# Fold matrix first on ScalarE's DMA queue, transposes of the state vectors behind the third fold tile

## The chip, the core and the metric

The kernel runs on one core of a Trainium2 chip. The metric is device time in microseconds (us) for one execution. The kernel before takes 340.8 us (median of 4 runs, 340.13 to 341.16).

## What is computed

Two mixers read the same input `x` (2048 x 1024, bf16), and a sigmoid gate blends their outputs.

```python
g = sigmoid((x * gate_w).sum(-1, keepdims=True))
# A: filter in the spectrum of both axes
a = irfft2(rfft2(x) * (w_r + 1j * w_i))
# B: diagonal complex state space over the sequence
dt = exp(log_dt);  Lam_bar = exp(dt * Lam)
Bu = x @ (((Lam_bar - 1) / Lam)[:, None] * Bmat).T
h[t] = Lam_bar * h[t - 1] + Bu[t]
b = 2 * (h @ Cmat.T).real + x * Dskip
out = g * a + (1 - g) * b
```

## The kernel before

All Fourier transforms are matrix products on TensorE (PE). The work falls into four stages.

**Fold, 0 to 27 us.** `x` comes in eight tiles of 512 KB on SyncE's queue (`load_x`, L208; called xt or CT in the profile). `fstage(jj)` (L467) handles one tile: VectorE (DVE) makes four sums and differences (L471 to L474, tile `eo`), GpSimd (POOL) fixes one column with four small instructions (L476 to L479). After every odd tile, PE multiplies the last two tiles by the fold matrix `FW_sb` in four fold tiles `ps_f` (L498 and L499, 16 column blocks with half of the sums each; a fold tile is eight matmuls of 256 columns), and ScalarE (ACT) copies each fold tile out in two instructions (L502, L503). So there are 16 fold tiles and 32 copies. `ps_f` has three buffers in PSUM.

**Scalars, beside the fold.** The state-space part needs small vectors (decay, angle, input scale). `vec8` holds the four vectors as 8 x 128; four PE transposes (L258, with `ident`) turn them into `vps`, and DVE copies them to `vec` and `gw1` (L272, L274). The generator `scalars()` (L307, `chain`) then runs eight short steps of instructions on 128 x 8 elements, mostly on DVE: step 1 has two exponentials and two sines on ACT, step 7 the Arctan (L351), step 8 `beta` (L355). Step 1 is emitted before the fold; then each `fstage` emits one more. When the steps are done, `tables(q)` (L369) makes the cosine and sine tables, the first of them from L377 to L390.

**Spectrum and state space, 27 to 156 us.** `fft_main` (L642) goes over 16 frequency groups (`fd`, `bf_w`, `w_mul`, `bi`), then does the inverse transforms; `ssm_all` (L736) is merged into it by hand.

**Output, to the end.** The product with `Cmat` (L836), the gate and the store.

The order on SyncE and GpSimd is the program's (`manual_schedule`, L190). On PE, DVE and ACT a planner sets the order beforehand, from estimated durations and from the emission order; on the chip each engine then works strictly in that order. Buffers are rings: tiles with the same tag share `bufs` slots, and a new tile waits until the slot's last reader is done. `vec8` and the `eo` of odd tiles share the tag "cu" with two slots, in the order `vec8`, `eo` of tile 1, `eo` of tile 3.

ScalarE's queue issues six loads at the start: `ident`, the four vectors, and `FW_sb` last (L194 to L198). The loads of both queues share eight completion semaphores in rotation; a load that gets a used semaphore waits on its queue until the earlier load with it has landed. The state-space weights come by DMA transposes (`load_BT`, `load_xT`), which start after a marker copy on DVE (L723) behind tile 3.

Of the kernel before, what the change touches and what calls it, by code (L numbers as in the profile page):

```python
# [22 lines left out]
P = 128  # L23
TC = 512
# [113 lines left out]
def kernel(  # L138
# [52 lines left out]


    FW_sb = BT[:, 7, 0, 0:4, :].rearrange("p a c -> p (a c)")
    nc.scalar.dma_start(out=ident, in_=cId)  # L194
    vec8 = rp.tile([8, 4, P], BF16, name="vec8", tag="cu")
    for i, src in enumerate((B_Lambda_re, B_Lambda_im, B_log_dt, gate_w)):
        nc.scalar.dma_start(out=vec8[:, i, :], in_=src.rearrange("(j p) -> j p", p=P))
    nc.scalar.dma_start(out=FW_sb, in_=cFW)  # L198

    warm = BT[:, 6, 0, 0:4, :].rearrange("p a c -> p (a c)")  # L200
    nc.vector.memset(warm, 0.0)
# [51 lines left out]
    xts.append(load_x(6))  # L253
    load_W(0)
    xts.append(load_x(7))
    vps = psU.tile([P, 4, 8], BF16, name="vps", tag="psu")
    for i in range(4):
        nc.tensor.transpose(out=vps[:, i, :], in_=vec8[:, i, :], identity=ident[0:8, 0:8])  # L258

    sp = cpool  # L260

# [7 lines left out]
        return scr[:, scr_n[0] - 1, :]  # L269

    vec = scr[:, 28:31, :]
    nc.vector.tensor_copy(out=vec, in_=vps[:, 0:3, :])  # L272
    gw1 = sp.tile([P, 8], BF16, name="gw1")
    nc.vector.tensor_copy(out=gw1, in_=vps[:, 3, :])  # L274
    gf = sp.tile([P, 16], FP32, name="gf")
    om_f = sp.tile([P, 16], FP32, name="om_f")
    lre, lim, ldt = vec[:, 0, :], vec[:, 1, :], vec[:, 2, :]
# [80 lines left out]
        yield  # L358

    chain = scalars()  # L360
    for _ in range(1):
        next(chain, None)

    tau_i = rp.tile([P, TC], I32, name="tau_i", tag="su")
    nc.gpsimd.iota(tau_i, pattern=[[1, TC]], base=0, channel_multiplier=0)
# [3 lines left out]
    def tables(q):  # L369
        xa = rp.tile([P, 2 * TC], FP32, name="xa", tag="cu")  # L370
        kk = rp.tile([P, 2 * TC], FP32, name="xa_k", tag="su")
        tq = tab[:, 2 * q:2 * q + 2]
        for jj in range(2):
            jb = 2 * q + jj
            xj, kj = xa[:, TC * jj:TC * (jj + 1)], kk[:, TC * jj:TC * (jj + 1)]
            if q < 1:
                nc.vector.tensor_scalar(out=xj, in0=tau_f, scalar1=thp[:, jb:jb + 1], scalar2=beta[:, jb:jb + 1],  # L377
                                        op0=ALU.mult, op1=ALU.add)
                yield
            else:  # L380
                nc.scalar.activation(out=xj, in_=tau_f, func=ACT.Identity, scale=thp[:, jb:jb + 1],
                                     bias=beta[:, jb:jb + 1])
            nc.vector.tensor_scalar(out=kj, in0=xj, scalar1=MAGIC, scalar2=-MAGIC, op0=ALU.add, op1=ALU.add)
            yield
            nc.vector.tensor_sub(out=xj, in0=xj, in1=kj)
            nc.vector.tensor_scalar(out=kj.bitcast(I32), in0=xj.bitcast(I32), scalar1=0x7FFFFFFF, scalar2=None,
                                    op0=ALU.bitwise_and)
            yield
            nc.scalar.activation(out=tq[:, jj, 0, :], in_=kj, func=ACT.Sin, scale=-TWO_PI_LO, bias=chpi)
            nc.scalar.activation(out=tq[:, jj, 1, :], in_=xj, func=ACT.Sin, scale=-TWO_PI_LO)  # L390
        nc.vector.tensor_scalar_mul(out=tq[:, :, 2, :], in0=tq[:, :, 1, :], scalar1=-1.0)
        yield


# [72 lines left out]
    def fstage(jj):  # L467
        xt = xts[jj]
        eo = (rp if jj % 2 else up).tile([P, 2, 2, 2, 256], BF16, name="eo", tag="cu" if jj % 2 else "u")
        if jj not in ():  # L470
            nc.vector.tensor_add(out=eo[:, :, 0, 0, :], in0=xt[:, :, 0:256], in1=xt[:, :, 512:768])  # L471
        nc.vector.tensor_sub(out=eo[:, :, 1, 0, :], in0=xt[:, :, 0:256], in1=xt[:, :, 512:768])  # L472
        nc.vector.tensor_add(out=eo[:, :, 0, 1, 1:256], in0=xt[:, :, 511:256:-1], in1=xt[:, :, 1023:768:-1])  # L473
        nc.vector.tensor_sub(out=eo[:, :, 1, 1, 1:256], in0=xt[:, :, 511:256:-1], in1=xt[:, :, 1023:768:-1])  # L474
        om = sm.tile([P, 2, 1], FP32, name="om")
        nc.gpsimd.tensor_add(out=eo[:, :, 0, 1, 0:1], in0=xt[:, :, 256:257], in1=xt[:, :, 768:769])  # L476
        nc.gpsimd.tensor_sub(out=om, in0=xt[:, :, 256:257], in1=xt[:, :, 768:769])
        nc.gpsimd.tensor_sub(out=eo[:, :, 1, 1, 0:1], in0=om, in1=eo[:, :, 1, 0, 0:1])
        nc.gpsimd.tensor_add(out=eo[:, :, 1, 0, 0:1], in0=om, in1=eo[:, :, 1, 0, 0:1])  # L479
        eos[jj] = eo  # L480
        for _ in range(1):
            next(chain, None)
        if jj % 2 == 0:
            return
        j0 = 2 * jj - 2
        for eo_i in range(2):
            for b in range(2):
                ps = psF.tile([P, 4, 2, P], FP32, name="ps_f", tag="ps")
                bs = slice(P * b, P * (b + 1))
                for jl in range(4):  # L490
                    jt = jj - 1 + jl // 2
                    v = eos[jt][:, jl % 2, eo_i]
                    if jt in () and eo_i == 0:
                        los = [xts[jt][:, jl % 2, 512 * h + P * b:512 * h + P * (b + 1)] for h in range(2)]
                    else:
                        los = [v[:, 0, bs]]
                    for i, lo in enumerate(los):
                        nc.tensor.matmul(ps[:, jl], lhsT=lo, rhs=FW_sb[:, 0:2 * P], start=(i == 0), stop=False)  # L498
                    nc.tensor.matmul(ps[:, jl], lhsT=v[:, 1, bs], rhs=FW_sb[:, P * (1 + eo_i):P * (3 + eo_i)],  # L499
                                     start=False, stop=True)  # L500
                q = 4 * eo_i + 2 * b
                nc.scalar.copy(out=FX[:, q, :, j0:j0 + 4], in_=ps[:, :, 0, :].rearrange("p j c -> p c j"))  # L502
                (nc.vector.tensor_copy if (jj, eo_i, b) in () else nc.scalar.copy)(  # L503
                    out=FX[:, q + 1, :, j0:j0 + 4], in_=ps[:, :, 1, :].rearrange("p j c -> p c j"))
                yield 1.0
# [110 lines left out]

    def gates():
        pg = psU.tile([P, TC], FP32, name="pg", tag="psu")
        gwT = fr.tile([P, 8, 32], BF16, name="gwT", bufs=1)
        nc.gpsimd.tensor_copy(out=gwT, in_=gw1.unsqueeze(2).to_broadcast([P, 8, 32]))  # L620
        for dblk in range(8):
            for c in range(NCH):
                nc.tensor.matmul(pg[32 * c:32 * (c + 1), :], lhsT=gwT[:, dblk, :], rhs=xT[:, dblk, TC * c:TC * (c + 1)],  # L623
                                 start=(dblk == 0), stop=(dblk == 7))
        lrow = fr.tile([P, 2, TC], BF16, name="lrow", bufs=1)
        nc.scalar.copy(out=lrow[:, 0, :], in_=pg)
        nc.vector.tensor_sub(out=lrow[:, 1, :], in0=pg, in1=lrow[:, 0, :])
        yield
        pc = psU.tile([P, 4, 4], FP32, name="pc", tag="psu")
        for q in range(4):  # L630
            for i in range(2):
                nc.tensor.matmul(pc[:, q, :], lhsT=lrow[:, i, P * q:P * (q + 1)], rhs=ident[:, 0:P:32],
                                 start=(i == 0), stop=(i == 1))
        gb = fr.tile([P, 16], BF16, name="gb", bufs=1)
        nc.scalar.activation(out=gb.rearrange("p (c q) -> p q c", q=4), in_=pc, func=ACT.Sigmoid)
        nc.vector.tensor_copy(out=gf, in_=gb)
        ob = fr.tile([P, 16], BF16, name="ob", bufs=1)
        nc.vector.tensor_scalar(out=ob, in0=gb, scalar1=-1.0, scalar2=1.0, op0=ALU.mult, op1=ALU.add)
        nc.vector.tensor_copy(out=om_f, in_=ob)
        yield  # L640

    def fft_main():  # L642
# [8 lines left out]
        for g in range(16):  # L651
            if g + 2 < 16:
                fd(g + 2)
                yield 1.2
            if g + 1 < 16:
                bf_w(g + 1)
                yield 1.0
            if 1 == 0 and g + 1 < 16:
                w_mul(g + 1)
            bi(g)  # L660
            if 1 == 1 and g + 1 < 16:
                w_mul(g + 1)
            if g + 4 < 16:
                load_M(g + 4)
            for f in sp_work.get(g, ()):
                f()
            yield 1.2
# [4 lines left out]
        for jj in range(9):  # L672
            if jj < 8:
# [6 lines left out]
                def mk_pm():  # L680
                    pm = fr.tile([P, 2, 2, 512], BF16, name="pm")
                    nc.vector.tensor_add(out=pm[:, :, 0, :], in0=yps[:, :, 0, :], in1=yps[:, :, 1, :])
                    nc.vector.tensor_sub(out=pm[:, :, 1, :], in0=yps[:, :, 0, :], in1=yps[:, :, 1, :])
                    pms[jj] = pm

                if -1 < 0 or jj == 0:
                    mk_pm()
                if jj == 5:
                    gt = gates()
                    next(gt)  # L690
                    yield 2.0
                if jj == 5 + 1:
                    next(gt)
                    yield 0.3
            if jj > 0:
# [204 lines left out]
```

## Time and profile before

| what | value |
|---|---|
| median of 4 runs | 340.8 us |
| the profiled execution's own time | 340.91 us |
| its span, first to last instruction | 339.0 us |
| PE busy | 321.3 us, 95% |
| DVE busy | 285.6 us, 84% |
| ACT busy | 191.3 us, 56% |
| POOL busy | 52.2 us, 15% |
| mean granted PE clock | 0.989 |

The span is what the profile's lines add up to; the 1.9 us between it and the execution's own time lie before the first and after the last instruction. Times in the lines count from the start of the span. A line of the timeline gives the start, the duration (instructions of one engine are pipelined, so durations overlap), engine, line, operation, tiles, and in brackets the idle time before it with what ended it. A "q" behind an engine marks its sequencer, such as the issue of a DMA.

### The profile page before, as it was taken

To read this page: it belongs to the slowest core of one execution; us is meant where nothing else is said; L and a number is where in the kernel's file an instruction comes from. 1 tells how busy PE (TensorE), PEld (TensorE's weight loads), DVE (VectorE), ACT (ScalarE), POOL (GpSimd) and SP (SyncE) were. 2 spreads that over 40 slices of the span, in tenths; PEclk is the share of its full clock that TensorE was granted. 3 is DMA by queue.
4 is the path that set the end of the run, shared out by engine and by line. 5 is a ranking of instruction groups with operands and counts; after the bars stand their busy time and mean duration, and the time that the engine had idled before them with its cause. 6 is when DMAs were issued, how large, how long until landed. Compare 5 with 4: busy or idle time off the path is not lost.

```text
span 339.0 us, 4984 instructions
## 1 busy us (share of the span) xinstructions
PE 321.3 (95%) x1813; PEld 174.7 (52%) x1845; DVE 285.6 (84%) x416; ACT 191.3 (56%) x269; POOL 52.2 (15%) x100
## 2 busy tenths in 40 slices
PE   6989989989979999999999999999999999999995
PEld 2765666756646566554444444444444444444442
DVE  4892799999979997999998999999999988972311
ACT  1999899989886877697252425341424425352200
POOL 4540322221301000000011002112022022111100
PEclk9899999999997999999999999999999999999999
DMA  7999999997597113023995054955675283977511
GB/s 253 383 181 232 182 253 194 226 233 151 152 203 142 62 62 126 31 95 140 241 217 178 21 166 82 259 96 131 148 155 145 74 218 95 258 223 228 159 48 45
DMA packets 70712, 54.97 MB, mean 162 GB/s; under 512 B 52768, under 2 KB 57888, under 8 KB 70688
## 3 DMA queue, kind: packets, MB, share of 16 engines
q1 hardware_dynamic: 64144, 38.75, 45.0%
q0 software_dynamic: 6192, 15.74, 21.2%
q8 instruction: 14, 0.23, 0.3%
q10 hardware_dynamic: 352, 0.17, 0.2%
q14 instruction: 10, 0.08, 0.1%
HBM read 21.61 MB, written 8.39 MB: 88 GB/s over the span
## 4 chain that ended last, share of the span: by engine, by line
PE 68%; issue 15%; DMA 7%; POOL 4%; DVE 3%; DVEq 0%; POOLq 0%
PE psy L836 32%; PE psu L412 26%; PE ps_id L589 5%; DMA W<-in_A_w_i_dram 4%; POOL W L246 4%; DMA xt<-in_A_x_dram 3%; PE ps_y L608 1%; PE ps_y L611 1%; PE ps_y L610 1%; PE ps_y L609 1%; DVE eo L471 1%; PE pg L623 1%; DVE eo L472 0%; DVE t L555 0%; DVE eo L473 0%
## 5 line engine op out<-in xcount | busy, mean ns | idle before, releaser
L412 PE MATMUL psu<-xT,BT 128*128 128x512 bf16 x489 | 117.2, 382 | 1.4 <-DMA xT<-in_A_x_dram 0.3
L412 PEld LDWEIGHTS <-BT 128*128 128x128 bf16 x512 | 50.2, 98 | 55.5 <-issue 1.8
L432 DVE TENSOR_TENSOR_SCAN su<-r_sb,carry,cu 128x512 bf16<-128x512 f32 x48 | 57.8, 1266 | 0.4
L414 ACT ACTIVATE u<-psu,rho 128x512 bf16<-128x512 f32 x32 | 22.1, 691 | 50.9 <-PE psu L412 48.4
L414 ACT ACTIVATE u<-psu,nrho 128x512 bf16<-128x512 f32 x32 | 22.1, 692 | 37.4 <-PE psu L412 37.4
L836 PEld LDWEIGHTS <-h 128*128 128x128 bf16 x256 | 25.0, 98 | 30.2
L843 DVE SCALAR_TENSOR_TENSOR o<-psy,om_f,xf 128x1024 bf16<-128x1024 f32 (+1 forms) x17 | 20.6, 1216 | 17.3 <-PE psy L836 17.3
L821 POOL DMA_DIRECT2D xf<-gac x16 | 16.3, 1019 | 118.0 <-ACT xf L820 118.0
L836 PE MATMUL psy<-big,h 128*128 128x512 bf16 x127 | 28.9, 379 | 0.1
L836 PE MATMUL psy<-CT,h 128*128 128x512 bf16 x125 | 28.6, 379 | 0.1
L818 ACT ACTIVATE gac<-gac,gf 128x1024 bf16<-128x1024 bf16 x16 | 18.2, 1140 | 17.6 <-DMA gac<-ya_scratch 17.6
L423 DVE TENSOR_TENSOR cu<-u,tab 128x2048 bf16<-128x2048 bf16 x16 | 19.5, 1218 | 2.3 <-ACT u L414 2.3
L814 DVE TENSOR_TENSOR xc<-xc,dsk_bc 128x1024 bf16<-128x1024 bf16 x16 | 10.9, 684 | 12.0 <-DMA xc<-in_A_x_dram 11.9
L836 PEld LDWEIGHTS <-xT 128*128 128x128 bf16 x128 | 12.5, 98 | 15.1
L836 PEld LDWEIGHTS <-big 128*128 128x128 bf16 x128 | 12.5, 98 | 15.1
L427 DVE TENSOR_TENSOR cu<-cu,su 128x2048 bf16<-128x2048 bf16 x16 | 19.6, 1228 | 0.4
L425 DVE TENSOR_TENSOR su<-u,tab 128x2048 bf16<-128x2048 bf16 x16 | 19.5, 1217 | 0.0
L515 PE MATMUL ps_d<-G_sb,big 128*128 128x256 bf16 (+3 forms) x128 | 18.9, 285 | 0.2 <-ACT X L542 0.2
L432 DVE TENSOR_TENSOR_SCAN su<-r_sb,cu 128x512 bf16<-128x512 f32 x16 | 18.7, 1209 | 0.1
L820 ACT ACTIVATE xf<-xc,om_f 128x1024 f32<-128x1024 bf16 x16 | 18.2, 1139 | 0.4 <-DVE o L843 0.4
L582 ACT CAST big<-ps_q 128x1024 bf16<-128x1024 f32 x16 | 16.3, 1021 | 2.9 <-PE ps_q L581 2.8
L589 PE MATMUL ps_id<-G_sb,big 128*128 128x256 bf16 (+3 forms) x128 | 17.4, 287 | 0.0
(169 smaller groups left out, 576.6 us busy)
## 6 DMA issues: line engine op xcount, KB each, us to landing
xf<-gac POOLq DMA_DIRECT2D x16, 512.0 KB, 6.2
ya_scratch<-ya SPq DMA_DIRECT2D x16, 256.0 KB, 2.0
xc<-in_A_x_dram SPq DMA_DIRECT2D x16, 256.0 KB, 3.8
gac<-ya_scratch SPq DMA_DIRECT2D x16, 256.0 KB, 3.7
out_dram<-o SPq DMA_DIRECT2D x15, 256.0 KB, 2.7
MM<-c_MM SPq DMA_DIRECT2D x16, 192.0 KB, 3.1
xt<-in_A_x_dram SPq DMA_DIRECT2D x4, 512.0 KB, 4.6
CT<-in_A_x_dram SPq DMA_DIRECT2D x4, 512.0 KB, 8.2
```

What stands on the lines that cost most here:

```text
L412: nc.tensor.matmul(psu, lhsT=BT[:, jb, ri, dblk, :], rhs=xT[:, dblk, TC * c:TC * (c + 1)], start=(dblk == 0), stop=(dblk == 7))
L414: nc.scalar.activation(out=u[:, jj, ri, :], in_=psu, func=ACT.Copy, scale=(nrho if ri else rho)[:, jb:jb + 1])
L423: nc.vector.tensor_mul(out=cu, in0=u, in1=tq[:, :, 0:1, :].to_broadcast(full))
L425: nc.vector.tensor_mul(out=su, in0=u[:, :, ::-1, :], in1=tq[:, :, 1:3, :])
L427: nc.vector.tensor_add(out=cu, in0=cu, in1=su)
L432: nc.vector.tensor_tensor_scan(out=su[:, jj, ri, :], data0=r_sb[:, jb:jb + 1].to_broadcast([P, TC]), data1=cu[:, jj, ri, :], initial=(0.0 ...
L515: nc.tensor.matmul(ps[:, lo:lo + w], lhsT=FX[:, q, 8 * g:8 * g + 8, :], rhs=G_sb[:, o:o + w], start=start, stop=stop, skip_group_check=True)
L589: nc.tensor.matmul(ps[:, lo:lo + w], lhsT=FX[:, q, :, j], rhs=G_sb[:, o:o + w], start=start, stop=stop, skip_group_check=True)
L818: nc.scalar.activation(out=gac, in_=gac, func=ACT.Copy, scale=gf[:, tb:tb + 1])
L820: nc.scalar.activation(out=xf, in_=xc, func=ACT.Copy, scale=om_f[:, tb:tb + 1])
L836: nc.tensor.matmul(psy[:, ds], lhsT=hs[c, jb // 2][:, jb % 2, ri, P * tq:P * (tq + 1)], rhs=CT[dh][:, jb, ri, :], start=(i == 0), stop=(i ...
L843: nc.vector.scalar_tensor_tensor(out=o[:, ds], in0=psy[:, ds], scalar=om_f[:, tb:tb + 1], in1=xfs[tb][:, ds], op0=ALU.mult, op1=ALU.add)
```

## The change

Two moves, with a third that follows from the second. The load of `FW_sb` becomes the first of the six on ScalarE's queue. The four transposes and the two copies behind them go into a function `vectors()`, which is called in `fstage(1)` after the third of its four fold tiles; `issue_after` ties the transposes behind that tile's last matmul on PE. The steps of `scalars()` are redistributed: step 1 right behind `vectors()`, then two at tile 2, two at tile 3, one each at tiles 4, 5 and 6.

```diff
     FW_sb = BT[:, 7, 0, 0:4, :].rearrange("p a c -> p (a c)")
+    nc.scalar.dma_start(out=FW_sb, in_=cFW)
     nc.scalar.dma_start(out=ident, in_=cId)
...
         nc.scalar.dma_start(out=vec8[:, i, :], in_=src.rearrange("(j p) -> j p", p=P))
-    nc.scalar.dma_start(out=FW_sb, in_=cFW)
...
-    vps = psU.tile([P, 4, 8], BF16, name="vps", tag="psu")
-    for i in range(4):
-        nc.tensor.transpose(out=vps[:, i, :], in_=vec8[:, i, :], identity=ident[0:8, 0:8])
...
-    nc.vector.tensor_copy(out=vec, in_=vps[:, 0:3, :])
     gw1 = sp.tile([P, 8], BF16, name="gw1")
-    nc.vector.tensor_copy(out=gw1, in_=vps[:, 3, :])
+
+    def vectors():
+        vps = psU.tile([P, 4, 8], BF16, name="vps", tag="psu")
+        for i in range(4):
+            nc.tensor.transpose(out=vps[:, i, :], in_=vec8[:, i, :], identity=ident[0:8, 0:8])
+        nc.vector.tensor_copy(out=vec, in_=vps[:, 0:3, :])
+        nc.vector.tensor_copy(out=gw1, in_=vps[:, 3, :])
...
     chain = scalars()
-    for _ in range(1):
-        next(chain, None)
...
         eos[jj] = eo
-        for _ in range(1):
+        for _ in range((0,0,2,2,1,1,1,0)[jj]):
             next(chain, None)
...
+                if jj == 1 and 2 * eo_i + b == 2:
+                    with tc.issue_after(last.ins):
+                        vectors()
+                    next(chain, None)
```

Everything else in the diff leaves the program as it is: conditions that are never or always true (`q >= 9`, `-1 >= 0`, `-1 < 0`, `if 0`), and two tiles of 16 columns, `gb` and `ob`, in another pool.

## The prediction

> **What bounds the kernel now.** I read the page first: PE is 95% busy over the span, so only time in which PE waits can be won, and that lies before 100 us. Then the table of windows over the fold, and over the stage behind it.
>
> ```profile
> 4.75:6.78 2.03, 0.70 (x4) 0.46 (x5) 1.43 (x4) 0.00 (x0) 1.27 (x4) 1.00 1.04 350
> 6.78:8.12 1.34, 0.95 (x6) 0.48 (x5) 1.33 (x6) 0.21 (x1) 0.99 (x4) 0.79 1.10 349
> 8.12:10.87 2.75, 2.75 (x13) 1.90 (x14) 2.19 (x12) 1.87 (x4) 2.32 (x8) 0.50 0.95 370
> 10.87:12.88 2.01, 1.64 (x14) 1.32 (x13) 1.93 (x9) 2.00 (x6) 1.59 (x6) 0.97 0.99 379
> 12.88:21.26 8.38, 8.31 (x68) 6.27 (x67) 7.84 (x42) 7.76 (x16) 3.62 (x16) 1.00 1.26 273
> 21.26:27.10 5.84, 4.55 (x36) 3.46 (x37) 4.87 (x13) 5.84 (x14) 0.97 (x4) 1.00 1.07 225
> 60.00:80.00 20.00, 18.37 (x141) 12.39 (x143) 19.86 (x37) 18.05 (x26) 5.83 (x10) 1.00 0.97 216
> ```
>
> The columns are length, then busy us and count of PE, PEld, DVE, ACT and POOL, granted clock, DMA share, GB/s. From 10.87 to 27.10 ACT is busy 15.60 of 16.23 us: the fold is ACT's. Before 8.12 ACT does next to nothing. From 60 to 80 DVE has 99%, PE 92%, ACT 90%: an order in which the three hand work to each other, so a shift of its start should run through it.
>
> Next, the timelines of ACT, PE and DVE and the DMA issues say what holds ACT back.
>
> ```profile
> 2.83 0.36 ACTq L198 DMA_DIRECT2D BT<-c_FW  x1
> 8.98 0.59 ACT L502 CAST big<-ps_f 128x512 bf16<-128x512 f32 x1 [1.76 <-PE ps_f L499]
> 10.17 1.28 ACT L313 ACT_TABLE_LOAD   x1
> 21.26 0.21 ACT L351 ACTIVATE scr<-scr 128x8 f32<-128x8 f32 x1 [0.62 <-DVE scr L349]
> 27.09 0.83 ACT L389 ACTIVATE tab<-xa_k,chpi 128x512 bf16<-128x512 f32 x1
> ```
> ```profile
> 6.16 0.60 PE L258 MATMUL vps<-ident,vec 8*128 8x8 bf16 x3 [1.15 <-DMA vec<-in_B_Lambda_im_dram]
> 6.78 0.38 PE L498 MATMUL ps_f<-BT,eo 128*128 128x256 bf16 x2
> 26.58 0.81 PE L412 MATMUL psu<-xT,BT 128*128 128x512 bf16 x2 [0.34 <-DMA xT<-in_A_x_dram]
> ```
> ```profile
> 4.90 0.42 DVE L471 TENSOR_TENSOR eo<-xt 128x512 bf16<-128x512 bf16 x1 [3.78 <-DMA xt<-in_A_x_dram]
> 6.79 0.18 DVE L272 CAST scr<-vps 128x24 f32<-128x24 bf16 x1 [0.46 <-PE vps L258]
> 10.78 0.43 DVE L471 TENSOR_TENSOR eo<-xt 128x512 bf16<-128x512 bf16 x1 [0.56 <-DMA xt<-in_A_x_dram]
> 22.59 0.99 DVE L377 TENSOR_SCALAR xa<-tau_f,ang,beta 128x512 f32<-128x512 f16 x2
> ```
> ```profile
> BT<-c_FW ACTq DMA_DIRECT2D x1, 128.0 KB, 3.9
> ident<-c_ident ACTq DMA_DIRECT2D x1, 32.0 KB, 3.5
> SPq L213 <- DMA ident<-c_ident: 2.7, 1, 2.7
> ```
>
> The fold matrix is issued at 2.83 and lands 3.9 us later, at 6.73; the first fold matmul runs at 6.78, though its sums were there at 4.90 + 0.42 = 5.32. Two gates stand side by side: the matrix, and the transposes until 6.76. The change lifts both. The last line is a wait of SyncE's own queue: the third x tile waits for the semaphore of `ident`.
>
> **The matrix first.** Issued at 0.72, it lands at 0.72 + 3.9 = 4.6 at its own latency; at `ident`'s 3.5, at 4.2. Both are ahead of 5.32, so the first matmul goes at about 5.35, 1.4 us earlier. The other half of the first fold tile needs tile 1's sums. DVE comes to those at 6.96, after the vector copies and 0.46 us of waiting for them; without these it goes on after tile 0, at 4.90 + 4 x 0.34 = 6.26, if tile 1 is there: issued at 1.18, about 5.0 to land, 6.2. So tile 1 and the end of the first fold tile move 0.7 us. ACT's first copy moves from 8.98 to between 8.0 and 8.3; I take 8.0, from the later rows' spacing of a fold tile, 8 x 0.109 us.
>
> The price is on the DMA side. 128 KB now runs beside x tile 0; at the 350 GB/s of the first window that is 0.37 us on its landing at worst, nothing at best, since the same bytes were moved by 6.73 anyway. SyncE's third x tile now waits for the matrix's semaphore instead of `ident`'s: it goes out at 4.2 to 4.6 instead of 4.28, 0 to 0.3 us. I take 0.1 of both, as tile 3, which DVE awaits at 10.78, is behind the same total of bytes.
>
> [...]
>
> **The transposes behind the third fold tile.** They cost PE 0.60 us for three, so 0.8 for four; PE is not the bound of the fold, and these 0.8 us delay only the fourth fold tile, which waits on ACT anyway. What they release comes later: `vec` at 6.97 becomes `vec` after the third fold tile. When that is depends on the clock. At full clock fold tiles 2 and 3 end at 8.0 + 2 x 0.87 = 9.7 and `vec` is there at 10.7. At half clock, as from 8.12 to 10.87, a matmul takes 0.213 us, a tile 1.7, the third ends near 11.0 and `vec` comes at 12.0.
>
> [...] I count nothing for it, and put 13 matmuls x 0.104 = 1.35 us into the low end.
>
> **The scalar steps.** Step 1 is 8 small DVE instructions with the two copies: between wide instructions each shifts the stream by 0.08 us, in series by 0.2, so 0.65 to 1.6 us. Before, they fill DVE's pauses (0.46 at 6.79, 0.56 at 10.78); now they fall behind tile 3, where DVE is busy to 22.6 without a break. The cover is ACT: DVE's first table input is done at about 25.8 and the first sine starts at 27.09, when ACT has finished the copies, 1.3 us of slack. I take 0.8, which it covers. ACT's own work is the same: the table load of 1.28 moves from 10.17 to a place where ACT waits for tile 3's sums. SyncE waits for nothing new on this side; POOL's L319 and L320 stand behind tile 2 instead of tile 0.
>
> **The sum**, on the profiled execution: first copy 8.98 to 8.0, -1.0; DMA +0.1; DVE's delay 0, covered; transposes 0, covered. ACT's end of the fold goes from 27.1 to 26.2. Then xT, which lands at 26.5, is next: PE's product L412 waited 0.34 for it, but the spectrum's `fd` does not need it, and ACT is full from 27 on. I pass on the whole 0.9, and 0.2 more for DVE's two pauses, which leave the stream of tiles 1 and 2. 340.91 - 1.1 = 339.8, and against the median of 340.8, 0.1 below that execution, 339.7.
>
> **Rivals.**
> 1. *Slower: tile 3 waits for `vec8`.* `eo` of tile 3 takes `vec8`'s slot, so its first DVE instruction waits for the last transpose. It decides if that ends after 10.78, so at the half clock: 11.0 + 0.8 = 11.8, DVE stands 1.0 us, and step 1's 0.65 to 1.6 come on top. DVE's stream ends 1.7 to 2.6 late; the Arctan, already 0.62 late in ACT's queue, holds the last six fold tiles' copies behind it. Less the 0.9 won: +0.8 to +1.7, 341.6 to 342.5; with the planner's order against it, 343. For it: the 0.50 clock in the row. Against: ACT may have the later tiles' copies placed ahead of the Arctan.
> 2. *No change: the transfers set the end of the fold.* The DMA share is about 1 throughout; xT lands at 26.5 and tile 3 at 10.76 whatever ACT does. The gain ends in a wait for them, 0 to -0.5: 340.5. The case that the matrix still lands after 6.5, in the crowd of the first loads, gives the same.
> 3. *More gained: the clock stays full.* -1.1 - 1.35: 338.3. The planner also re-orders PE, DVE and ACT behind the fold; by the waits there (2.8 us for the filter's loads, 5 to 7 for products) I allow 1 us either way.
>
> **How the numbers follow.** What a measurement of this kernel can tell from no change is about 0.2%, 0.7 us. Forecast, with rival 3: 0.54, 338.3 to 340.1, likeliest 339.7. Rival 1: 0.32, 341.5 to 343. Rival 2: 0.14. So faster 0.54, same 0.14, slower 0.32. Both signs hold much, so the range reaches over most of rival 1, to 342.6, and down to 338.3; the likeliest case alone is 338.3 to 340.1.
>
> **What would show it.** Right: the matrix lands before 5, the first L498 at about 5.4, ACT's first L502 near 8.0, its last L503 near 25.7, the first sine near 26.2. Wrong: tile 3's L471 on DVE waits for PE L258, or the idle time before the Arctan grows past 1 us, or the first L498 still waits for the matrix. If the fold ends early and the end does not move, the wait is to be sought at xT or the filter's loads.

## The result and the profile after

The changed kernel takes 341.56 us (median of 53 runs) where the kernel before took 340.70 (79 runs of the same series): ratio 1.002, 95% interval 1.001 to 1.003. It is slower by 0.3 to 1.0 us. The prediction was 339.7, faster; the time lies in the range and the sign is wrong. (A ratio here and below is taken over all runs of both kernels and is not the quotient of the two medians.)

The profiled execution after took 340.95 us with a span of 339.2, against 340.91 and 339.0 before. Lines after L194 carry other numbers now: the fold's sums are L472 to L475, its matmuls L501 and L502, its copies L509 and L510, the transposes L274, the Arctan L354, the sines L390 and L391, the first spectral matmuls (`fd`) L522, their copy to `X` on ACT L534, the state-space product L413.

First the fold in the timeline of the kernel after: start, duration, engine, line, operation, tiles, and in brackets the idle time before it.

```profile
5.40 0.42 DVE L472 TENSOR_TENSOR eo<-xt 128x512 bf16<-128x512 bf16 x1 [4.27 <-DMA xt<-in_A_x_dram]
5.88 0.61 PE L501 MATMUL ps_f<-BT,eo 128*128 128x256 bf16 x2 [0.69 <-DVE eo L472]
8.78 0.59 ACT L509 CAST big<-ps_f 128x512 bf16<-128x512 f32 x1 [4.19 <-PE ps_f L502]
11.10 0.25 PE L274 MATMUL vps<-ident,vec 8*128 8x8 bf16 x4
11.39 0.18 DVE L275 CAST scr<-vps 128x24 f32<-128x24 bf16 x1 [1.27 <-PE vps L274]
11.58 0.42 DVE L472 TENSOR_TENSOR eo<-xt 128x512 bf16<-128x512 bf16 x1
14.72 1.28 ACT L316 ACT_TABLE_LOAD   x1
24.91 0.21 ACT L354 ACTIVATE scr<-scr 128x8 f32<-128x8 f32 x1 [0.57 <-DVE scr L352]
28.36 0.69 ACT L391 ACTIVATE tab<-xa 128x512 bf16<-128x512 f32 x1
```

The first fold matmul no longer waits for the matrix: it goes at 5.88, when `eo` is there (6.78 before). But x tile 0 came 0.50 later (5.40 against 4.90), and the matmuls ran at half speed until 10.2 (0.213 us from start to start, 0.109 behind it; see the last section), so the first copy gained 0.20 only. The transposes came at 11.10, tile 3's first sum at 11.58 right behind the copies of `vps` (10.78 before), the Arctan 3.65 later (21.26 before), and ACT came to its first sine, behind the last copy of the fold, at 28.36 instead of 27.09.

The same stretches in the table of windows after: length, busy us and count of PE, PEld, DVE, ACT and POOL, granted clock, DMA share, GB/s.

```profile
4.75:6.78 2.03, 1.28 (x6) 0.30 (x5) 1.38 (x5) 0.00 (x0) 1.16 (x4) 1.00 0.92 286
8.12:10.87 2.75, 2.75 (x17) 2.03 (x16) 1.57 (x6) 1.67 (x4) 1.43 (x5) 1.00 1.02 376
10.87:12.88 2.01, 2.01 (x22) 1.57 (x20) 1.10 (x7) 1.70 (x6) 0.98 (x4) 1.00 1.00 346
12.88:21.26 8.38, 6.55 (x55) 5.10 (x54) 8.11 (x37) 8.14 (x18) 4.69 (x14) 1.00 1.23 296
21.26:27.10 5.84, 4.75 (x39) 3.48 (x38) 4.91 (x25) 5.24 (x13) 1.61 (x8) 1.00 0.98 198
```

ACT is no longer full: from 10.87 to 27.10 it is busy 15.08 us of 16.23, against 15.60 before. From 8.12 to 10.87 DVE is busy 1.57 us where it was 2.19: it stands before tile 3.

The DMA issues and SyncE's waits after (KB each and median us to landing; total us, times, longest):

```profile
BT<-c_FW ACTq DMA_DIRECT2D x1, 128.0 KB, 4.2
ident<-c_ident ACTq DMA_DIRECT2D x1, 32.0 KB, 5.2
SPq L213 <- DMA BT<-c_FW: 3.3, 1, 3.3
```

The matrix lands at 0.72 + 4.2 = 4.9. `ident`, behind it, takes 5.2 instead of 3.5, and SyncE now waits 3.3 us for the matrix's semaphore instead of 2.7 for that of `ident`.

Then the place where the spectrum begins, in the timeline of the kernel after:

```profile
26.90 0.38 PE L413 MATMUL psu<-xT,BT 128*128 128x512 bf16 x1 [0.22 <-DMA xT<-in_A_x_dram]
27.11 0.82 PE L522 MATMUL ps_d<-G_sb,big 128*128 128x512 bf16 x5
27.98 0.59 PE L413 MATMUL psu<-xT,BT 128*128 128x512 bf16 x2
28.41 0.38 PE L522 MATMUL ps_d<-G_sb,big 128*128 128x256 bf16 x2
28.64 0.38 PE L413 MATMUL psu<-xT,BT 128*128 128x512 bf16 x1
28.85 0.27 PE L522 MATMUL ps_d<-G_sb,big 128*128 128x256 bf16 x1
29.16 1.01 ACT L534 CAST X<-ps_d 128x1024 bf16<-128x1024 f32 x1
```

PE first waits for `xT`, with one state-space matmul at the head of its queue. Only behind that come the eight matmuls of the first spectral group, four more state-space matmuls among them (the profile has lost the record of one). The first copy to `X` is at 29.16; it was at 27.97 before. Before, five of the eight (L515) stood ahead of the wait for `xT`, and three were left after it. Around the line of L412 at 26.58 that the prediction shows, the timeline of before has:

```profile
25.43 0.82 PE L515 MATMUL ps_d<-G_sb,big 128*128 128x512 bf16 x5
27.66 0.27 PE L515 MATMUL ps_d<-G_sb,big 128*128 128x256 bf16 x1
27.97 1.01 ACT L527 CAST X<-ps_d 128x1024 bf16<-128x1024 f32 x1
```

(The expectations below count from the landing of `xT`, 0.14 ahead of the end of the wait: 2.40 after, 1.52 before.) So the planner put one state-space matmul ahead of five spectral ones; that a moved estimate of the fold's end made it do so is likely and not shown. It also put another sine ahead of that copy on ACT (L391 for L389). Behind this place the engines' orders are the same in both kernels, as far as the records go.

### The profile page after: what moved, and what is told of

The parts are those of the page before. It is cut to its first block, busy times and chain, and to the rows that moved or that the text cites. A ratio compares the mean times of both kernels' runs of the same rounds, so it can differ in the third digit from the quotient of the medians.

```text
span 339.2 us, 4983 instructions
## 1 busy us (share of the span) xinstructions
PE 320.3 (94%) x1813; PEld 173.7 (51%) x1845; DVE 286.5 (84%) x416; ACT 191.4 (56%) x269; POOL 51.9 (15%) x100
## 4 chain that ended last, share of the span: by engine, by line
PE 67%; issue 16%; DVE 5%; DMA 5%; POOL 5%; ACT 1%; DVEq 0%; POOLq 0%
PE psy L858 32%; PE psu L413 25%; POOL W L246 4%; PE ps_id L596 3%; DMA W<-in_A_w_i_dram 2%; DMA xt<-in_A_x_dram 1%; DMA W<-in_A_w_r_dram 1%; PE ps_y L615 1%; PE ps_y L618 1%; PE ps_y L617 1%; PE ps_y L616 1%; PE ps_f L502 1%; DVE su L433 1%; PE pg L637 1%; PE ps_f L501 1%
## 5 line engine op out<-in xcount | busy, mean ns | idle before, releaser
L413 PE MATMUL psu<-xT,BT 128*128 128x512 bf16 x489 | 116.1, 379 | 1.3 <-DMA xT<-in_A_x_dram 0.2
L413 PEld LDWEIGHTS <-BT 128*128 128x128 bf16 x512 | 50.0, 98 | 54.7 <-issue 0.9
L522 PE MATMUL ps_d<-G_sb,big 128*128 128x256 bf16 (+3 forms) x128 | 18.9, 285 | 0.3 <-ACT X L549 0.2
L501 PE MATMUL ps_f<-BT,eo 128*128 128x256 bf16 x64 | 15.9, 291 | 2.2 <-ACT big L510 1.5
```

Of the source, the lines that this page charges most:

```text
L413: nc.tensor.matmul(psu, lhsT=BT[:, jb, ri, dblk, :], rhs=xT[:, dblk, TC * c:TC * (c + 1)], start=(dblk == 0), stop=(dblk == 7))
L522: nc.tensor.matmul(ps[:, lo:lo + w], lhsT=FX[:, q, 8 * g:8 * g + 8, :], rhs=G_sb[:, o:o + w], start=start, stop=stop, skip_group_check=True)
```

## The experiments

Four theories. **R**: the loss is this order. The first `X` copy (the start of the spectrum on ACT) stands a fixed distance behind the end of the wait for `xT`, and a state-space matmul at the head of PE's queue holds spectral matmuls that do not need `xT`. **S**: the scalar steps, now late, hold ACT's fold end, and that sets the start, as in rival 1. **L**: the loads. The matrix first pushes the other loads back. **W**: an earlier start is given back at the wait for the filter's third load. Each ratio below is to the kernel before, run beside it on the same chip, with its 95% interval; each kernel has 12 runs, and one of its executions was profiled.

### The two moves alone

The matrix first, in the kernel before:

```diff
+    nc.scalar.dma_start(out=FW_sb, in_=cFW)
     nc.scalar.dma_start(out=ident, in_=cId)
```

> The kernel before with the load of the fold matrix first on ScalarE's queue, and nothing else moved. Theory S (the scalar steps come too late behind the third fold tile, the loads cost little): 0.5 us faster to 0.2 us slower than before; the transposes still stand ahead of the first fold matmul, at about 7 us; first sine within 0.5 us of 27.1. Theory L (the matrix beside x tile 0 pushes the x tiles and the small loads back): 0.5 to 1.0 us slower than before, first fold instruction on VectorE at 5.4 instead of 4.9, first sine at 27.6 or later.

Measured: 340.21 against 339.34, ratio 1.0035 [1.0013, 1.0056]. Its timeline:

```profile
7.74 0.17 PE L258 MATMUL vps<-ident,vec 8*128 8x8 bf16 x1
7.95 0.18 DVE L272 CAST scr<-vps 128x24 f32<-128x24 bf16 x1 [1.69 <-PE vps L258]
8.12 0.42 DVE L471 TENSOR_TENSOR eo<-xt 128x512 bf16<-128x512 bf16 x1
10.14 0.58 ACT L502 CAST big<-ps_f 128x512 bf16<-128x512 f32 x1 [1.77 <-PE ps_f L499]
```

The time is what L asked for, but not by the way that its expectation named: x tile 0 was hardly pushed back (its first sum is at 4.83 and not at 5.4; 4.90 in the first profile of before, 4.67 in c0 on this chip). The loads behind the matrix on its own queue were: the first transpose runs at 6.57 instead of 4.83 and the last at 7.74 instead of 6.58, DVE stands 1.69 us for it with tile 1's sums behind, and the first copy is 1.16 late. The first sine is at 27.93 and the `X` copy at 28.56. Lifting one of two gates that stand side by side made the other one worse.

The transposes late, the matrix last as before (the changed kernel with the first line of the diff undone):

> The changed kernel with the load of the fold matrix last again: the engines' order is that of the changed kernel but for this load. Theory S: 0.6 to 1.3 us slower than before; VectorE stands ahead of tile 3 until the vector copies, the Arctan comes after 24 us, the first sine near 28. Theory L: within 0.3 us of before or faster, as x tile 0 lands at 4.9 again and the first sine comes at 27.1 or earlier.

Measured: 1.0028 [1.0007, 1.0050]. The first copy is at 8.04; in the changed kernel run again (below) it is at 8.06. So in these executions the gain at the first copy is there without the matrix's new place, and that place adds nothing to it. The loss is there too without the matrix first, so it is not L's alone.

### Parts of the late scalar steps

`vec8` in a place of its own, so that tile 3's sums do not wait for the transposes:

```diff
-    vec8 = rp.tile([8, 4, P], BF16, name="vec8", tag="cu")
+    vec8 = BT[0:8, 6, 1, 0:4, :]
```

> The changed kernel with the state vectors' staging tile in a place of its own (a part of the state-space weights that is loaded much later), so that tile 3's sums no longer need its slot. The planner then puts tile 3's four VectorE instructions ahead of the vector copies. If the slot is what costs: tile 3 starts at 10.0 to 10.8, the first sine comes back to 27.3 or earlier, time within 0.3 us of before. If the late start of the scalar steps costs by itself: tile 3 early, but the Arctan still after 24 us and the first sine after 27.9, 0.4 to 1.0 us slower than before.

Measured: 1.0030 [1.0010, 1.0050]. Tile 3's sums start at 9.79 and no longer wait, the planner then puts the copies of `vps` behind tile 3 (11.20), and nothing is won. The Arctan is at 23.89 and the first sine at 27.33, so neither of the two expected pictures came whole. Rival 1's wait for the slot is real but is not the loss. The `X` copy is at 28.23, 2.27 behind the end of the wait for `xT` (25.96): the start is only 0.3 to 0.6 later than in the profiles of before, and yet the 12 runs are as slow as those of the changed kernel.

One scalar step moved from tile 6 to tile 7:

```diff
-        for _ in range((0,0,2,2,1,1,1,0)[jj]):
+        for _ in range((0,0,2,2,1,1,0,1)[jj]):
```

> The changed kernel with step 8 of the scalars emitted behind tile 7 instead of tile 6: on GpSimd alone four instructions move behind tile 7's column fix, which stood 2.7 us behind them in the changed kernel. If that wait holds the last fold tiles: TensorE no longer idles at 22.3 to 23.2, the first sine comes 0.4 to 0.7 us earlier than 28.4, time 0.3 to 0.6 us below the changed kernel. If the Arctan's place in ScalarE's queue holds them: the idle time on TensorE goes, the Arctan stays near 24.9, and the time is that of the changed kernel within 0.2 us.

Measured: 1.0056 [1.0031, 1.0081], the slowest of all, and why is not shown. PE no longer idles at 22.3 to 23.2; the Arctan is at 24.30 and the first sine at 27.74, but the first `X` copy is at 29.47, 2.27 behind the end of the wait for `xT` (27.20). So the late steps do not set the start of that profile. It is no typical one either: it took 339.27, the shortest of the 12 runs, and had no wait for the sixteenth load.

### The kernels again, and the filter's third load

Both kernels as they are:

> The kernel before itself, as a control on the chip that the next three share: a ratio of 1.000 within its interval under every theory; first sine near 27.1, a wait of about 1 us for the filter's third load at 41 us.

> The changed kernel on the same chip: 0.3 to 1.1 us slower than before. The first sine is 1.0 to 1.5 us later than in the control, but the filter's multiplication of group 2 at most 0.4 us later: the wait for the filter's third load takes up the rest. If that wait is not what takes it up, the shift of 1.0 to 1.5 us is still there at group 5.

Measured: 0.9993 [0.9966, 1.0020] and 1.0021 [0.9998, 1.0043]. In this pair the fold of the changed kernel ran at full speed (its matmuls of 256 columns start 0.109 us apart), that of before at half speed until 9.8 (0.213 us apart; last section), so the pair shows the early start of the fold at its best. First copy 8.06 against 8.77, 0.71 ahead, 0.2 to 0.3 of it by the clock (an estimate: the first fold tile's last two matmuls took 0.61 us in c0 and 0.39 in c1). But the fold is not ended sooner: the first sine is at 26.88 against 26.58, 0.30 later, where the expectation said 1.0 to 1.5. From first copy to first sine ACT needs 18.82 us against 17.81. On the way it waits 0.21 for a fold tile and 0.61 for the Arctan's input, and the first exponential, which before lay ahead of the copies, now lies among them; the sixth fold tile's copy is only 0.10 ahead (15.28 against 15.38), and the Arctan, at 23.44 instead of 20.74, stands among the last copies. The Arctan before (c0) and after (c1):

```profile
20.74 0.21 ACT L351 ACTIVATE scr<-scr 128x8 f32<-128x8 f32 x1 [0.30 <-DVE scr L349]
23.44 0.21 ACT L354 ACTIVATE scr<-scr 128x8 f32<-128x8 f32 x1 [0.61 <-DVE scr L352]
```

The pair also answers W. The `X` copy is 1.24 later (28.87 against 27.63), and DVE's products with the filter are still later by 1.34 at the third group (41.27 against 39.93), the sixth (54.71 against 53.37) and by 1.35 at the fifteenth (96.89 against 95.54). Neither execution waited for the third load, and the shift goes through whole.

The filter's third load issued early on SyncE into free space, in the kernel before and after:

```diff
             load_BT(3)
+            load_W(2)
...
-        w = Wtiles[g % 2]
+        w = W2t if g == 2 else Wtiles[g % 2]
```

> The kernel before with the filter's third load (group 2) sent early on SyncE's queue into a place of its own, so that it no longer starts behind the multiplication of group 0; the engines' order is otherwise that of before. If the wait for this load stands on the path: it disappears at 41 us, group 3 comes about 0.9 us earlier, 0.4 to 1.0 us faster than before. If the load is not on the path: within 0.3 us of before.

> The changed kernel with the filter's third load sent early in the same way. If the wait for this load hides most of the delay of the fold: the gap to the early-load form of before is the whole delay, 1.0 to 1.5 us at group 5 and 0.9 to 1.5 us at the end; against before itself 0 to 0.9 us slower. If something else hides it: the gap at the end stays at 0.3 to 1.0 us.

Measured: 1.0021 [0.9999, 1.0043] and 1.0042 [1.0020, 1.0065]. Both are 0.2% above the kernels that they come from. The edit seems to cost more than it frees, so it cannot say what that wait is worth. Inconclusive.

### The order on PE

The first state-space product tied behind the last matmul of the first spectral group. First in the kernel before and in the changed one:

```diff
+                with (tc.issue_after(fd_last[0].ins) if (c, q, jj, ri) == (0, 0, 0, 0) else nullcontext()):
                     for dblk in range(8):
                         nc.tensor.matmul(psu, lhsT=BT[:, jb, ri, dblk, :], rhs=xT[:, dblk, TC * c:TC * (c + 1)],
...
-        mm(7, 768, 256, False, True)
+        fd_last[g] = mm(7, 768, 256, False, True)
```

> The kernel before with the first state-space product tied behind the last matmul of the first spectral group on TensorE; the other engines' order is that of before. Theory R (the first spectral group's copy hangs on the landing of the transposed x, because a state-space matmul stands ahead of part of that group in TensorE's queue): the copy comes 0.1 to 0.5 us earlier than in the control (27.63), no longer at a fixed distance from that landing; 0 to 0.5 us faster. Theory S (the end of the fold on ScalarE sets it): no change beyond 0.1 us at that copy, time that of before within 0.3 us.

> The changed kernel with the same tie; the other engines' order is that of the changed kernel. Theory R: the first spectral group's copy comes at 27.6 to 28.0 instead of 28.9 to 29.2, 0.9 us or more earlier; the kernel is 0.5 to 1.0 us faster than the changed one, within 0.4 us of before. Theory S: that copy moves by less than 0.3 us, and the kernel stays 0.5 to 1.1 us slower than before.

Measured: 1.0004 [0.9986, 1.0022] and 1.0003 [0.9976, 1.0031]. The tie is nothing in the kernel before. The tied changed kernel shows no slowdown, though its interval still holds 1.002. Its `X` copy is at 27.49, 0.54 behind the first sine at 26.95.

That pair had no untied changed kernel on its chip. So both, side by side:

> The changed kernel as it is, on the same chip as the next run. Both theories: 1.002 of before (0.3 to 1.2 us more). In its profile the first spectral copy on ACT stands 2.40 us behind the landing of xT.

> The changed kernel with the first state-space product tied behind the first spectral group on PE, on the same chip as the changed kernel itself. Theory R (the place of those matmuls costs what the change lost): the copy stands 0.55 to 0.65 behind the first sine and no longer a fixed 2.40 behind xT; 0.5 to 0.9 us less than the changed kernel, ratio to before 0.9995 to 1.0005. Theory S (the late end of the fold is the loss): the same time as the changed kernel within 0.2 us, ratio 1.002.

Measured: 1.0031 [1.0007, 1.0056] and 1.0034 [1.0014, 1.0055]. The times say the opposite of the pair before: no gain from the tie. The traces are clear. The kernel before run again (c0), the changed one (s_after), the tied one (s_after_tied), each in the timeline around the end of the fold:

```profile
24.91 0.82 PE L515 MATMUL ps_d<-G_sb,big 128*128 128x512 bf16 x5
26.25 0.81 PE L412 MATMUL psu<-xT,BT 128*128 128x512 bf16 x2 [0.52 <-DMA xT<-in_A_x_dram]
26.58 0.83 ACT L389 ACTIVATE tab<-xa_k,chpi 128x512 bf16<-128x512 f32 x1
27.33 0.27 PE L515 MATMUL ps_d<-G_sb,big 128*128 128x256 bf16 x1
27.63 1.01 ACT L527 CAST X<-ps_d 128x1024 bf16<-128x1024 f32 x1 [0.23 <-PE ps_d L515]
```
```profile
26.91 0.38 PE L413 MATMUL psu<-xT,BT 128*128 128x512 bf16 x1 [1.42 <-DMA xT<-in_A_x_dram]
27.13 0.82 PE L522 MATMUL ps_d<-G_sb,big 128*128 128x512 bf16 x5
27.17 0.69 ACT L391 ACTIVATE tab<-xa 128x512 bf16<-128x512 f32 x1
28.87 0.27 PE L522 MATMUL ps_d<-G_sb,big 128*128 128x256 bf16 x1
29.17 1.01 ACT L534 CAST X<-ps_d 128x1024 bf16<-128x1024 f32 x1 [1.31 <-PE ps_d L522]
```
```profile
25.00 0.82 PE L525 MATMUL ps_d<-G_sb,big 128*128 128x512 bf16 x5
25.98 1.27 PE L525 MATMUL ps_d<-G_sb,big 128*128 128x512 bf16 x9 [0.16 <-ACT big L511]
26.74 0.69 ACT L391 ACTIVATE tab<-xa 128x512 bf16<-128x512 f32 x1
27.08 1.89 PE L414 MATMUL psu<-xT,BT 128*128 128x512 bf16 x8
27.28 1.05 ACT L537 CAST X<-ps_d 128x1024 bf16<-128x1024 f32 x1
```

Before, the copy follows the end of the wait for `xT` by 27.63 - 26.25 = 1.38 us; in the changed kernel by 29.17 - 26.91 = 2.26, and by the same 2.26 in its first profile (26.90, 29.16), where ACT ended the fold 1.19 later (28.36 against 27.17). So ACT's late end cost that profile nothing beyond the order on PE. But it was close: with the tie the copy comes 0.54 behind the first sine, which by that sine's 28.36 is 28.90, so in the first profile the late fold end (S) alone would have held the start to within 0.26 of where the order (R) did. In s_after and c1, with the first sine at 27.17 and 26.88, the order alone decides. PE waits 1.42 us for `xT` here with work at hand, and ACT then 1.31 for PE. With the tie PE does not wait for `xT` at all and the copy is 1.89 earlier. The lines show the order kept: nothing of L522 goes until the one L413 has gone, at 26.91, while in the tied kernel the same five matmuls (L525 there) go at 25.00.

Most of the 1.89 went into the waits for the filter's loads. DVE's products of the third group and of the sixteenth, in the tied kernel:

```profile
41.15 0.69 DVE L565 TENSOR_TENSOR t<-X,W 128x1028 bf16<-128x1028 bf16 x1 [1.36 <-DMA W<-in_A_w_i_dram]
101.32 0.69 DVE L565 TENSOR_TENSOR t<-X,W 128x1028 bf16<-128x1028 bf16 x1 [2.36 <-DMA W<-in_A_w_i_dram]
```

1.36 at the third load, 2.36 at the sixteenth. In s_after they are 0 and 2.01. The profiled span differs by 0.4 us only. The wait for the third load also stood in the first profile of before (1.02 at 41.36), and not in r_after, which started about as early (27.49). The sixteenth load is no slack that takes up a shift: GpSimd issues its second half behind an earlier product, and the issue moves with the start (91.51 in c0, 92.85 in c1). Its wait follows from the load's own time, 7.86 and 7.42 us from issue to use there, 8.44 in s_after and 8.78 in s_after_tied.

These two waits and the start give nearly the whole span. "Other" is the span less the three; all are us of the profiled execution, and the span of a kernel moves with the sum of the three columns. In the twelve profiles that the table leaves out, "other" runs from 307.4 to 308.8.

| kernel | first `X` copy | wait, third load | wait, sixteenth load | span | other |
|---|---|---|---|---|---|
| before | 27.97 | 1.02 | 1.81 | 339.0 | 308.2 |
| before again (c0) | 27.63 | 0 | 1.43 | 337.0 | 307.9 |
| before, tied (r_before) | 27.72 | 0 | 0.90 | 336.8 | 308.2 |
| after | 29.16 | 0 | 1.89 | 339.2 | 308.1 |
| after again (c1) | 28.87 | 0 | 0.99 | 337.9 | 308.0 |
| after, third time (s_after) | 29.17 | 0 | 2.01 | 339.3 | 308.1 |
| after, tied (r_after) | 27.49 | 0 | 1.78 | 337.7 | 308.4 |
| after, tied (s_after_tied) | 27.28 | 1.36 | 2.36 | 338.9 | 307.9 |

The three changed profiles start the spectrum at 29.07 on average, the two of before in its own order at 27.80: 1.27 later. Of that 0.88 is the order on PE (2.26 - 1.38), the rest a later landing of `xT` (26.67 against 26.28 on average). In the first profile of after, the fold's end would have taken 0.62 of the 0.88 without the order. The two tied ones start it at 27.39. That much is shown at the start. The sum of the two waits runs from 0.90 to 3.72 us between these executions, which is more than the effect, and whether the tie raises them or s_after_tied met long ones by chance is not settled.

The order put into the kernel before, by itself (the first four matmuls of that product emitted ahead, the spectral group tied behind them):

```diff
+    for dblk in range(4):
+        m0 = nc.tensor.matmul(psu0, lhsT=BT[:, 0, 0, dblk, :], rhs=xT[:, dblk, 0:TC], start=(dblk == 0), stop=False)
...
-        fd(0)
+        with tc.issue_after(m0.ins):
+            fd(0)
```

> The kernel before, with one thing of the change's side effect put in by hand: the first four matmuls of the state-space product (L412, which wait for xT) stand ahead of all eight matmuls of the first spectral group on PE; the fold matrix, the transposes and the scalar steps stay as before. The planner then also puts two more sines ahead of the first spectral copy on ACT. Theory R (the first spectral copy hangs on the landing of xT, because the in-order PE queue holds the spectral matmuls behind the state-space ones): copy at xT's landing + 4 x 0.22 + 8 matmuls (0.96) + about 0.55 = + 2.40, where before had + 1.52, so about 0.9 us later, the products with the filter about 0.9 later, and the time up by 0.6 to 1.0 us, ratio 1.002 to 1.003. Theory S (ACT's end of the fold sets the start, the place of the matmuls is nothing): copy 0.6 us behind the first sine as before, plus at most 0.85 for the two sines ahead of it only if those are what it waits for; ratio 1.000 if the order of PE is no cause.

Measured: 1.0010 [0.9994, 1.0025]; the sign of R, but not told from no change. Its timeline:

```profile
25.78 1.02 PE L778 MATMUL psu<-xT,BT 128*128 128x512 bf16 x3 [0.93 <-DMA xT<-in_A_x_dram]
26.64 1.15 PE L516 MATMUL ps_d<-G_sb,big 128*128 128x512 bf16 x8
27.50 0.81 ACT L389 ACTIVATE tab<-xa_k,chpi 128x512 bf16<-128x512 f32 x1
28.11 1.11 ACT L528 CAST X<-ps_d 128x1024 bf16<-128x1024 f32 x1
```

The copy follows the wait's end by 2.33, near R's 2.26, but partly by luck. The matmuls were done at 27.79, 2.01 behind the wait's end, and ACT still had the third sine from 27.50, so the last 0.3 us are ACT's.

### Looking for a version that beats both

The tied changed kernel with `vec8` in a place of its own:

> The changed kernel with the tie, and the staging tile of the state vectors in a place of its own. Theory R: first spectral copy about 0.9 us earlier than with the own place alone (28.23), near 27.4 to 27.9 as the fold's end allows; time within 0.4 us of before, and 0.3 to 0.9 us faster than with the own place alone. Theory S: first sine near 27.3 and the spectral copy near 28.2 as with the own place alone, 0.5 to 1.0 us slower than before.

Measured: 1.0018 [0.9995, 1.0041]. Again the slot is not shown to be worth anything.

The tied one with the transposes behind the first fold tile (`== 0` for `== 2`), on two chips:

> The changed kernel with the tie, and the transposes behind the first fold tile instead of the third. If a late start of the scalar steps is what delays the fold's end: vector copies at or before 10 us and the Arctan a microsecond or more earlier than in the changed kernel (23.4 on this chip's profile), the first sine at 26.0 to 26.6; the first spectral copy at 26.8 to 27.4; 0 to 0.8 us faster than before. If VectorE's order alone sets the steps' start: Arctan and first sine as with the tie alone, time as with the tie alone.

> The changed kernel with the vectors' transposes behind the first fold tile instead of the third, and the first state-space product tied behind the first spectral group on PE; run again on another chip because its ratio of 0.9988 lay inside its interval. If the early start of the fold reaches the end once the tie is there, 0.9985 to 0.999; if the gain of the first run was chance, 1.000 to 1.001.

Measured: 0.9988 [0.9969, 1.0007] and 1.0002 [0.9980, 1.0024]. The profiles show why one value is not to be trusted: the first had the first `X` copy at 27.89 and waited 0.47 for the sixteenth load (span 336.3); the second had it at 27.47, earlier, and waited 3.08 (span 338.7). "Other" is 308.0 and 308.1.

With the slot, and with the matrix last:

> As the run with the transposes behind the first fold tile and the tie, with vec8 in a buffer of its own, so that tile 3's sums don't wait for the transposes. With the transposes that early, tile 3's sums should not have waited anyway: same time as that run within 0.1%, 0.998 to 0.9995. If the shared slot still costs, 0.2 to 0.3 us less, near 0.998.

> As the run with the transposes behind the first fold tile and the tie, but with the fold matrix last of the six loads as before. If the matrix first is worth anything by itself, the first copy is later and the time 0.1 to 0.3% above that run. If the crowd of the first loads decides (each load pushed ahead pushes the others back), xT lands about 0.3 earlier, ident and the vectors 0.4 to 2 earlier, and the time is the same or 0.1% less: 0.9975 to 0.9985.

Measured: 1.0014 [0.9993, 1.0035] and 1.0012 [0.9991, 1.0033]. Neither differs from the run that it was to be told from.

No version is shown to beat the kernel before. Over the seven tied variants of the change the ratios run from 0.9988 to 1.0034, mean 1.0010; over the four untied ones with the same steps (c1, s_after, e2, e4) from 1.0021 to 1.0031, mean 1.0028. The difference, 0.6 us, has the sign of R and two thirds of its 0.88, but the variants are not the same kernel otherwise, they ran on different chips, and the one pair on one chip shows none of it. So the order on PE is shown as the cause of the late start, and not as the cause of the longer time.

## Why the prediction was wrong

**The matrix first.** Landing before 5 was right (4.88). The price on the DMA side was mis-sized: 0.1 was taken for tile 0 and the third tile, and it was 0.50 and 0.62 in the first profile, 0.35 and 0.60 in the pair c0 and c1 (tile 0's first sum 4.67 to 5.02; the third tile's issue 4.05 to 4.65). Tile 3, by which the small price was argued, landed earlier in the first profile (9.88, 10.76 before) and later in the pair (9.67 against 9.22). For tile 0 the 0.37 that the prediction worked out as the worst was nearer than the 0.1. The small loads behind the matrix paid more: `ident` landed 2.0 later in the first profile, and in the run of the matrix alone the last transpose came 1.16 later; there DVE's wait for it (1.69, 0.46 before) makes up the delay of the first copy.

**The first copy.** 8.0 was taken; with the full clock (matmuls 0.109 us apart) it came at 8.06 (c1) and 8.33 (s_after); in the first profile (0.213 apart) at 8.78. The transposes cost 0.25 us for four, not 0.8.

**Tile 3 and the clock.** Rival 1's mechanism came in the first profile much as it was worked out: last transpose near 11.3, tile 3 at 11.58 (11.8 was put), fold end +1.27 (+0.8 to +1.7). That is partly luck: by the rival's own figures, two fold tiles of 1.7 behind 8.0 end at 11.4 and not near 11.0, and the transposes took less. And though the median of 341.56 lies at the edge of rival 1's range, its wait is not shown as the reason: with `vec8` in a place of its own the wait is gone and the ratio is 1.0030. Rival 3's condition, a full clock in the fold, came in c1 and s_after, and nothing of its -1.35 was there. That term was the author's estimate from the two spacings, 0.213 and 0.109 us; no run shows that the change sets the clock, for the changed kernel ran its fold's start at 0.213 in the first profile and at 0.109 in c1 and s_after. Both were taken for the switch between gain and loss, and these runs do not show the time to hang on either.

**"ACT's end of the fold goes from 27.1 to 26.2."** This step failed. The sum took the lead of the first copy through 16 us to the last one, since ACT was busy 15.60 of 16.23. In the first profile ACT came to the first sine at 28.36; and in c1, with a full clock, the lead of 0.71 was a delay of 0.30 at the end (26.88 against 26.58). The mis-sized term is the one at "0, covered": the scalar steps, put behind tile 3, were taken to delay DVE by 0.8 us. DVE came to the tables 2.91 later in the first profile (25.50 against 22.59) and 1.96 in c1 (24.03 against 22.07), and the Arctan came 3.65 and 2.70 later, with the last seven copies behind it. Between first copy and first sine ACT stood idle 1.57 us after and 0.65 before, 0.92 in c1 and 0.33 in c0. Of the 0.59 more in c1, 0.31 is the wait for the Arctan and 0.21 one for a fold tile; in the first profile the wait for the Arctan is no longer than before (0.57 against 0.62), and the new ones stand earlier. The rest of the lost lead, 0.42 in c1, lies in the new order on ACT and is not shown apart. The place for it was in the prediction (rival 1 says that the Arctan holds the last copies behind it), but priced for the half clock alone.

**"I pass on the whole 0.9."** This step failed too, and it is the one that made the start of the spectrum late where the clock was full. The prediction saw PE's 0.34 us of waiting for `xT` and dismissed it because the spectrum does not need `xT`. It does not, but its matmuls stood behind one that does, and PE took them in that order (in s_after none of them went in its 1.42 us of waiting). The start was `xT`'s end of wait plus the matmuls queued behind it: 1.38 us before, 2.26 after. No gain upstream could pass while `xT` landed no earlier, and the planner's new order lost 0.88 more. Rival 2 named `xT` as the end that is next, with 0 to -0.5 and no term for the order. The prediction did allow 1 us either way for the planner; it should have stood in a rival of its own with this place. What was right is the passing on behind the start: the shift at the `X` copy went through to the fifteenth group whole (c0 and c1). That this step set the sign of the time is not shown, since tying the order back gained nothing in the pair on one chip.

**The end.** A later start by 1.27 on average in the profiles stands beside 0.86 in the medians. Between the two in any one execution lie the two filter waits, together 0 (the run with the last step late) to 3.72 us (s_after_tied). In the first pair the wait of 1.02 for the third load stood in before alone and hid most of the later start: the spans there differ by 0.2 us. Which part of the 0.86 is the order, which the fold's end and which the loads stays open.

## What to carry to other kernels

When an engine works in order, a short wait of one instruction is the wait of everything queued behind it, whether that needs the data or not (here PE stood 1.42 us with work at hand): look up what stands behind the waiting instruction before passing a gain through. After an edit upstream of a planner, the order at the next hand-over is part of the change and has to be costed, and where the gain is small, pinned. And before two gates side by side, check that lifting the one does not delay the other: here the matrix first held the transposes' loads back.

## What had not been expected of the hardware

The time of one load from issue to use varies by 3 us between executions. The second half of the filter's sixteenth load goes out 0.6 us behind the first half. In the run with the last step late that is at 93.42, and its first user starts at 99.77 without a wait, so the load took at most 6.35 us. In the first-tile kernel run again it is at 91.41, and the user starts at 100.92 behind a wait, 9.51 us later. Two executions of the changed kernel itself had 7.42 (c1) and 8.44 (s_after). The line of the longest, in its timeline:

```profile
100.92 0.69 DVE L565 TENSOR_TENSOR t<-X,W 128x1028 bf16<-128x1028 bf16 x1 [3.08 <-DMA W<-in_A_w_i_dram]
```

The column of the granted clock showed 1.00 in the fold of the kernel after, and yet its matmuls of 256 columns start 0.213 us apart until 10.2 and 0.109 apart behind it. So it is in c0, where the column shows 1.00 and the matmuls are 0.213 apart until 9.8. Three that follow one another in the timeline of c0:

```profile
8.74 0.42 PE L498 MATMUL ps_f<-BT,eo 128*128 128x256 bf16 x1
8.95 0.42 PE L499 MATMUL ps_f<-BT,eo 128*128 128x256 bf16 x1
9.17 0.42 PE L498 MATMUL ps_f<-BT,eo 128*128 128x256 bf16 x1
```

In before, the column and the rows agree (0.50, and 0.213 us from matmul to matmul, from 8.12 to 10.87). The slow stretches lie in another place from run to run, 7.6 to 11.0 and again from 103.1 in before, up to 10.2 in after, none behind 6.5 in the folds of c1 and s_after. The pause of PE ahead of the fold does not decide it: it was 0.69 us ahead of the first fold matmul in the first profile after and 0.56 in s_after, the same kernel, and only the former went on at 0.213 us a matmul. What does decide it is not shown.
